# Windowed attention and an ELU layer on one core: a new start order, dummy matmuls, and scores of two groups together

## Chip, core and metric

The kernel runs on one core of a Trainium2 chip. The metric is the device time of one execution in microseconds (us). Matrix products run on TensorE (PE; PEld is its weight load), elementwise work on VectorE (DVE), ScalarE (ACT) and GpSimd (POOL); SyncE (SP), ACT and POOL also issue DMAs.

## What is computed

Attention over 8 batches, 8 heads, 576 positions and 64 values per head, in which a position sees only its neighbours at a distance of up to 32; then a layer of 512 to 2048 values with an ELU, and one back to 512, over all 4608 tokens. Inputs and output are float32.

```python
B, H, S, D = 8, 8, 576, 64
scores = q @ k.transpose(0, 1, 3, 2) / sqrt(D)
scores = where(abs(pos[:, None] - pos[None, :]) <= 32, scores, -1e9)
attn = softmax(scores)
x = (attn @ v).transpose(0, 2, 1, 3).reshape(B * S, H * D)
h = x @ w_in                                  # 4608 x 2048
g = where(h > 0, h, exp(minimum(h, 0)) - 1)
out = g @ w_out                               # 4608 x 512
```

## The kernel before

**Units, groups and tiles.** Attention is cut into units of 64 query positions, 9 per batch and 72 in all; a group `G[i]` is two neighbouring units (37 groups, since the first two batches end with a single one). A group goes through these steps. `QK` makes the scores (16 matmuls for two units, contracting over 64 partitions, even heads on partitions 0-63 and odd heads on 64-127) into the PSUM tile `psS` of two banks. `SM` takes the exponentials of the whole tile on ACT (L406). `MK` multiplies by the band masks on DVE (L419). `AV` multiplies by v, with a column of ones for the sum (`psO`, L431). `RN` divides by the sum (L445, L447), and `X` transposes the result to `xt`, through PSUM and a copy (`XT`, `X`) for the first nine groups and by a DMA transpose afterwards.

The layer takes tiles of units, `sizes = [2, 2, 2, 3, 4, 3] + [8] * 7`. `H` is the hidden product (L487) into `psH`, which has three banks; `pack` of the small tiles puts several blocks of 128 hidden values into one bank. `EX` takes the exponential on ACT (L496), `FF` forms its negative part on ACT or DVE (`fact` chooses; L506, L508), and `GG` joins both to `g_sb` on DVE (L514, L517). `Y` is the output product in four parts for each chunk of 128 tokens (L532), alternately into `psY` and `psT` from chunk 6 on; `YC` copies it on ACT and `OUT` stores it. The eight PSUM banks are: psS 2, psO 1, psT 1, psH 3, psY 1.

**Loads.** SP loads q, k and v in blocks `L(b, nm, j)` of up to 128 positions, float32, into staging tiles (`stg`, four for v; `stp`, four for pairs of k and q). Casts to bfloat16 are `CV` for v and `C`, `C2` for k and q. For batch 0 the first half of k and q is transposed on TensorE (`T`) and copied out (`TT`, by `E`). The second half of batch 0 and all of batch 1 come in another way: POOL issues casting DMAs (`LR`) which put runs of six positions on one partition, 48 partitions per half of the heads; `TR` transposes them on TensorE in pieces of 48 by 64, and `ER` copies them to their place. Batch 0 takes 4 such transfers, batch 1 takes 8. From batch 2 on, SP's DMA transposes (`XB`) do it. The weights are cast by POOL's DMAs too, in four chunks each (`WI` for w_in, `WO` for w_out). Chunk c of w_in serves hidden blocks 4c to 4c+3, chunk c of w_out part c of each output chunk.

**What sets the order.** Every step is an operation of a planner, `Plan`, with an engine, an estimated duration, a rank, dependencies, and counted resources (PSUM banks, staging tiles, a ring of SP transfers, eight POOL transfers at a time). The planner plays the program through with its estimates: whenever an engine is free it takes the ready operation of lowest rank. The order in which operations start in that play is the order in which instructions are written, and each engine and queue then runs its own in that order. Ranks follow the unit (`PER = 4` per unit); attention has `LEAD = 36` ahead of the hidden layer, 9 units. POOL's queue at the start is the list `LINE` (L636): identity, masks, a `wait` (a one-element copy that reads a loaded block, `GATE`, L643: v's block 0), then weights and `LR`. SP's first eleven loads follow `FIRST` (L634). A small memset, `GT`, holds back the loads of batch 1 until a w_out chunk is in, and those of batch 2 until a k transfer of batch 1 is in.

Of the kernel before, what the change touches and what calls it, by code (L numbers as in the profile page):

```python
# [20 lines left out]
class Plan:  # L21
# [12 lines left out]
    BEGIN = {"POOL": 1.35, "SP": 0.8}  # L34
    QLAT = {"S": 1.2, "A": 1.2, "P": 2.2}

    def __init__(self, held):
        self.ops = {}
        self.held = dict(held)
        self.acq, self.rel, self.late = {}, {}, {}  # L40

    def op(self, name, eng, dur, rank, deps, fn, dma=None, acq=None,
           rel=None, late=0.0):
        assert name not in self.ops, name
        self.late[name] = late
        self.ops[name] = (eng, dur, rank, tuple(deps), fn, dma)
        if acq:
            self.acq[name] = acq if isinstance(acq, list) else [acq]
        if rel:
            self.rel[name] = rel  # L50

    def run(self):
# [7 lines left out]
        free, ready = {}, {}  # L60
        for n, o in ops.items():
            free.setdefault(o[0], self.BEGIN.get(o[0], 0.7))
            ready.setdefault(o[0], {})
            if left[n] == 0:
                ready[o[0]][n] = 0.0
# [4 lines left out]
        import heapq  # L70

        held = dict(self.held)

        def finish(n, t):
            done[n] = t
            if n in self.rel:
                r, k = self.rel[n]
                held[r] += k
                for e in free:
                    heapq.heappush(events, (t + self.LAT, 1, e))  # L80
            for u in users.get(n, ()):
                left[u] -= 1
                if left[u] == 0:
                    ue = ops[u][0]
                    r = max(done[d] + (0.0 if ops[d][0] == ue and ops[d][5] is None
                                       else self.LAT) for d in ops[u][3])
                    ready[ue][u] = r
                    heapq.heappush(events, (max(r, t), 1, ue))

        now = 0.0  # L90
        for e in free:
            heapq.heappush(events, (free[e], 1, e))
        while len(order) < len(ops) or events or any(rings.values()):
# [4 lines left out]
            if nxt is not None and (te is None or now + nxt <= te):  # L98
                now += nxt
                for q in rings.values():  # L100
                    if q:
                        q[0][1] -= nxt / per
                        if q[0][1] <= 1e-9:
                            h = q.pop(0)
                            for a, k in self.acq.get(h[0], ()):
                                if a == "ring":
                                    held[a] += k
                                    for e in free:
                                        heapq.heappush(events, (now, 1, e))
                            heapq.heappush(events, (now + self.DLAT + self.late[h[0]],  # L110
                                                    0, h[0]))
# [7 lines left out]
            _, kind, x = heapq.heappop(events)  # L119
# [13 lines left out]
            cand = [(ops[n][2], n) for n, r in rs.items() if r <= now + 1e-9  # L133
# [3 lines left out]
            n = min(cand)[1]  # L137
# [7 lines left out]
            heapq.heappush(events, (free[e], 1, e))  # L145
            if dma is not None:
                ring, pk, ns = dma
                heapq.heappush(events, (now + self.QLAT[ring], 2, (
                    ring, [n, float(pk), ns / 1000.0])))
            else:  # L150
                lag = self.PLAT - self.LAT if e == "PE" else 0.0
                heapq.heappush(events, (now + dur + lag, 2, n))
# [3 lines left out]
        self.start, self.done, self.order = start, done, order  # L156
        for n in order:
            ops[n][4]()
# [3 lines left out]
def kernel(  # L162
# [23 lines left out]
    RUN = 6  # L186
    HT = S // (2 * RUN)
# [10 lines left out]
    NXT = 3  # L198
    NST = 4
# [52 lines left out]
    def L(b, nm, j, eng):  # L252
# [7 lines left out]
        live["L", b, nm, j] = t  # L260


    def GT(b, nm, j):
        t = room(b, nm, j)
        nc.vector.memset(t[96:97, 0:1], 0.0)
        live["G", b, nm, j] = t
# [4 lines left out]
    def WAIT(b, nm, j):  # L271
        nc.gpsimd.tensor_copy(spot[64:65], live["L", b, nm, j][64:65, 0:1])
# [70 lines left out]
    def runs(b, nm, half):  # L343
        x = "kq".index(nm) + 2 * half
        n = HP * RUN * D
        if b == 0:
            o = (4 + 2 * "kq".index(nm) + 8 * half) * GC
            t = g_sb.rearrange("p a c -> p (a c)")[:, o:o + n]
        elif x == 3:
            t = qkT[2][:, 1].rearrange("p a c -> p (a c)")[:, 0:n]  # L350
        else:
            t = vw[2].rearrange("p a h d -> p (a h d)")[:, x * n:x * n + n]
        return t.rearrange("p (a r d) -> p a r d", a=HP, r=RUN)

    def LR(b, nm, half, two):
        src = SRC[nm][b].rearrange("(a two) s d -> two a s d", two=2)[two][
            :, half * (S // 2):(half + 1) * (S // 2)]
        nc.gpsimd.dma_start(
            out=runs(b, nm, half)[64 * two:64 * two + HT].rearrange(
                "p a r d -> p a (r d)"),  # L360
            in_=src.rearrange("a (p r) d -> p a (r d)", r=RUN))

    def TR(b, nm, half, part, bank):
        pool = {"psH": psH_p, "psT": psT_p}[bank]
        pt = pool.tile([128, 2, RUN, HT], BF16, name=bank, tag=bank)
        src = runs(b, nm, half)
        for a in range(2):
            for r in range(RUN):
                for p0 in (0, 64):
                    nc.tensor.transpose(  # L370
                        pt[p0:p0 + 64, a, r, :],
                        src[p0:p0 + HT, 2 * part + a, r, :],
                        ident[p0:p0 + HT, p0:p0 + HT])
        live["TR", b, nm, half, part] = pt

    def ER(b, nm, half, part, eng):
        w = qT[b] if nm == "q" else kT[b][:, :, WIN:WIN + S]
        dst = w[:, 2 * part:2 * part + 2, half * (S // 2):(half + 1) * (S // 2)]
        copy(eng, dst.rearrange("p a (g r) -> p a g r", r=RUN),
             live.pop(("TR", b, nm, half, part)).rearrange("p a r g -> p a g r"))  # L380
# [8 lines left out]

    def QK(i):  # L390
        psS = psS_p.tile([128, 2, 2, HP, QB], FP32, name="psS", tag="psS")
        for s, u in enumerate(G[i]):
            b, qb = divmod(u, NQB)
            for h in range(H):
                hp, base = h // 2, 64 * (h % 2)
                nc.tensor.matmul(  # L396
                    psS[:, h % 2, s, hp, :],
# [3 lines left out]
        live["S", i] = psS  # L401

    def SM(i):
        pu = pup.tile([128, 2, 2, HP, QB], BF16, name="pu", tag="pu")
        n = len(G[i])
        nc.scalar.activation(pu[:, :, 0:n], live.pop(("S", i))[:, :, 0:n],  # L406
                             AX.Exp, scale=SCALE)
        live["U", i] = pu
# [12 lines left out]
    def AV(i, g):  # L421
# [3 lines left out]
        else:  # L425
            o = psO_p.tile([128, HP, VW], FP32, name="psO", tag="psO")
# [8 lines left out]
        live["O", i, g] = o  # L435

# [30 lines left out]
    def XE(i):  # L467
        dst, pt = live.pop(("XT", i))
        nc.scalar.copy(dst, pt)
# [29 lines left out]
    def fact(t, fo):  # L499
        return fo // pack(t) % 2 == 1 if t < NTA else fo % 4 != 1  # L500
# [47 lines left out]
    for t, n in enumerate(sizes):  # L548
        for u in range(p0, p0 + n):
            tof[u] = t  # L550
            if u == G[gof[u]][0]:
# [6 lines left out]
    LL, CC, XX = 36, 18, 14  # L558
    RING, XBT = 2.2, 1.3
    LATE = {("L", 0, "v", 3): 5.0, ("L", 0, "v", 4): 5.0}  # L560
# [3 lines left out]
              "sp": NSP, "cb": NCB, "swq": 8, "ring": RING})  # L564
# [18 lines left out]
    def prank(i):  # L583
        return PER * G[i][0] - LEAD

# [36 lines left out]
    for i in range(NVB):  # L622
        P.op(("zvw", i), "DVE", 1.1, -1970 + i if not i else -910 + i,
             [("TR", 1, nm, half, part) for nm in "kq" for half in range(2)
              for part in range(2)] if i == 2 else [], lambda i=i: z_vw(i))
# [3 lines left out]
    def group_of(b, nm, j):  # L629
        if nm == "q":  # L630
# [5 lines left out]
    LINE = [("id",), ("mask",), ("wait",), ("WI", 0), ("WI", 1), ("0kB",), ("0qB",),  # L636
            ("WI", 2), ("WI", 3), ("WO", 0), ("WO", 1),
            ("WO", 2), ("1kA",), ("1qA",), ("WO", 3), ("1kB",), ("1qB",)]
    CVE = {(0, 0): "DVE", (0, 1): "ACT", (1, 0): "DVE", (1, 1): "ACT",
           (1, 2): "DVE", (2, 0): "ACT", (2, 1): "ACT", (2, 2): "DVE",  # L640
           (3, 0): "DVE", (3, 1): "ACT", (3, 2): "ACT", (4, 0): "DVE",
           (4, 2): "ACT"}
    GATE = ("v", 0)  # L643
    rk = -2000.0
    for x in LINE:
        rk += 1
        if x[0] == "wait":
            P.op(x, "POOL", 0.1, rk, [("L", 0) + GATE], lambda: WAIT(0, *GATE))
# [8 lines left out]
        else:  # L657
            b, nm, half = int(x[0][0]), x[0][1], "AB".index(x[0][2])
            for two in range(2):
                P.op(("LR", b, nm, half, two), "POOL", 0.6, rk + 0.1 * two, [("wait",)],  # L660
                     lambda b=b, nm=nm, half=half, two=two: LR(b, nm, half, two),
# [232 lines left out]
```

## Time and profile before

| | |
|---|---|
| median of 3 runs | 323.94 us (323.45 to 326.56) |
| the profiled execution | 323.2 us, span of its instructions 321.4 us |
| PE busy | 298.2 us, 93% of the span, 2867 matmuls |
| DVE, ACT, POOL busy | 201.0 (63%), 215.7 (67%), 109.1 us (34%) |
| first matmul | 5.38 us |
| last matmuls | end at 317.6 us |
| chain that ended last | PE 75%, DMA 14%, DVE 4%, issue 3%, ACT 2% |
| SP's queue | 142304 packets, 35.53 MB |
| POOL's queue | 6720 packets, 5.97 MB |

The page divides the span into 40 slices of 8 us; a digit is the busy share of an engine in tenths. A busy PE may still be slow inside: its matmuls are pipelined, and at a lower clock they last longer. Some matmul records are missing in a trace, so that a group of four may show as three. POOL's casting DMAs are counted with the bytes that they write, half of what they read.

### The profile page before, as it was taken

The numbers are of one execution on the slowest core, as the hardware profiler recorded it, in microseconds if no ns is written. First come the engines' busy times: TensorE is split into PE (matmuls) and PEld (weight loads), VectorE is DVE, ScalarE is ACT, GpSimd is POOL, SyncE is SP. The second block draws the span as 40 slices with busy tenths as digits, with TensorE's granted clock in tenths as the row PEclk, the third lists the DMA queues.
The fourth block names the chain that finished last, engine by engine and source line by source line (L and its number), as shares of the span: only waits on it lengthen the run. The fifth ranks groups of instructions, "written<-read, shape, count | busy, mean of one in ns | idle before, by whom it ended". The sixth has DMA issues, their size and how long they took to land.

```text
span 321.4 us, 7525 instructions
## 1 busy us (share of the span) xinstructions
PE 298.2 (93%) x2867; PEld 166.8 (52%) x2908; DVE 201.0 (63%) x447; ACT 215.7 (67%) x357; POOL 109.1 (34%) x160
## 2 busy tenths in 40 slices
PE   1698799999999998999999999999999999999995
PEld 1486666677754454444444444444444444444442
DVE  5755768797856698566666667667666666444400
ACT  4659565577867786866677777766777766667611
POOL 3642337855445543545346434552000000000000
PEclk9999999999999999999999999999999999999999
DMA  8999999999999989989999898997111111100021
GB/s 192 184 197 206 197 207 232 216 207 186 197 235 206 271 161 192 223 181 229 173 246 213 202 216 216 219 210 168 52 50 51 49 51 51 46 35 33 34 100 65
DMA packets 154244, 51.42 MB, mean 160 GB/s; under 512 B 143200, under 2 KB 149600, under 8 KB 154208
## 3 DMA queue, kind: packets, MB, share of 16 engines
q1 hardware_dynamic: 142304, 35.53, 58.5%
q0 software_dynamic: 6720, 5.97, 11.5%
q10 hardware_dynamic: 5184, 9.44, 8.5%
q8 instruction: 23, 0.38, 0.5%
q14 instruction: 13, 0.11, 0.1%
HBM read 36.70 MB, written 9.44 MB: 144 GB/s over the span
## 4 chain that ended last, share of the span: by engine, by line
PE 75%; DMA 14%; DVE 4%; issue 3%; ACT 2%; another core or an unknown queue 1%; SPq 1%; POOL 0%; ACTq 0%; DVEq 0%; POOLq 0%
PE psH L487 32%; PE psY L532 19%; PE psT L532 14%; DMA w_out_sb<-in_moe_w_out_dram 5%; PE psO L431 5%; DMA vw<-in_k_dram 4%; DMA w_in_sb<-in_moe_w_in_dram 3%; PE psS L396 3%; DMA st<-in_v_dram 1%; PE psO L532 1%; DVE g_sb L514 1%; DVE pm L419 1%; DVE xs L447 1%; DMA xt<-xs 1%
## 5 line engine op out<-in xcount | busy, mean ns | idle before, releaser
L487 PE MATMUL psH<-xt,w_in_sb 128*128 128x512 bf16 (+3 forms) x824 | 148.6, 317 | 1.4 <-DVE qk L278 0.5
L496 ACT ACTIVATE e<-psH 128x512 f32<-128x512 f32 (+1 forms) x148 | 86.1, 585 | 72.7 <-PE psH L487 63.2
L487 PEld LDWEIGHTS <-w_in_sb 128*128 128x128 bf16 x832 | 70.6, 100 | 48.2 <-issue 1.3
L514 DVE SCALAR_TENSOR_TENSOR g_sb<-f,psH 128x512 bf16<-128x512 bf16 (+1 forms) x106 | 70.2, 665 | 24.5 <-ACT f L506 23.9
L532 PEld LDWEIGHTS <-g_sb 128*128 128x128 bf16 x576 | 53.3, 98 | 58.7
L532 PE MATMUL psY<-w_out_sb,g_sb 128*128 128x512 bf16 x299 | 78.7, 379 | 2.1 <-issue 1.3
L278 POOL CAST vw<-st 64x512 bf16<-64x512 f32 (+3 forms) x98 | 62.8, 641 | 22.1 <-DMA st<-in_v_dram 16.9
L506 ACT ACTIVATE f<-e 128x512 bf16<-128x512 f32 (+1 forms) x106 | 65.5, 618 | 2.6
L419 DVE TENSOR_TENSOR pm<-pu,masks 128x512 bf16<-128x512 bf16 x72 | 35.2, 528 | 34.7 <-ACT pu L406 34.7
L532 PE MATMUL psT<-w_out_sb,g_sb 128*128 128x512 bf16 x213 | 55.0, 379 | 1.4 <-issue 1.3
L278 POOL CAST cb<-sp 128x1024 bf16<-128x1024 f32 (+1 forms) x30 | 31.7, 1056 | 65.5 <-DMA sp<-in_q_dram 60.3
L406 ACT ACTIVATE pu<-psS 128x1024 bf16<-128x1024 f32 (+1 forms) x37 | 36.9, 996 | 3.9 <-PE psS L396 3.8
L431 PEld LDWEIGHTS <-pm 128*128 128x128 bf16 x576 | 26.9, 99 | 17.0 <-DVE pm L419 3.6
L431 PE MATMUL psO<-vw,pm 128*128 128x65 bf16 x552 | 29.9, 195 | 2.4 <-DVE pm L419 1.6
L447 DVE TENSOR_TENSOR xs<-psO,rc 128x256 bf16<-128x256 f32 (+1 forms) x71 | 30.1, 424 | 2.5
L517 DVE TENSOR_TENSOR g_sb<-psH,f 128x512 bf16<-128x512 f32 (+1 forms) x42 | 28.5, 678 | 3.2
L445 DVE RECIPROCAL rc<-psO 128x4 f32<-128x4 f32 (+1 forms) x71 | 12.9, 182 | 24.4 <-PE psO L431 24.1
L508 DVE TENSOR_SCALAR f<-e 128x512 bf16<-128x512 f32 (+1 forms) x42 | 20.4, 488 | 6.1 <-ACT e L496 6.1
L396 PEld LDWEIGHTS <-qk 64*128 64x128 bf16 x576 | 11.1, 96 | 12.9 <-issue 11.4
L396 PE MATMUL psS<-qk 64*128 64x64 bf16 x576 | 15.4, 194 | 1.2 <-DVE qk L278 0.5
L538 ACT COPY y<-psY 128x512 f32<-128x512 f32 x20 | 11.4, 572 | 5.8 <-PE psY L532 5.8
L276 ACT COPY qk<-psH 128x576 bf16<-128x576 bf16 (+2 forms) x10 | 5.8, 590 | 7.9 <-PE psH L370 3.9
(52 smaller groups left out, 84.6 us busy)
## 6 DMA issues: line engine op xcount, KB each, us to landing
out_dram<-y ACTq DMA_DIRECT2D x36, 256.0 KB, 2.6
sp<-in_k_dram SPq DMA_DIRECT2D x26, 256.0 KB, 3.9
sp<-in_q_dram SPq DMA_DIRECT2D x26, 256.0 KB, 4.0
st<-in_v_dram SPq DMA_DIRECT2D x24, 256.0 KB, 4.1
st<-in_v_dram SPq DMA_DIRECT2D x16, 192.0 KB, 3.9
w_in_sb<-in_moe_w_in_dram POOLq DMA_DIRECT2D x4, 512.0 KB, 12.0
w_out_sb<-in_moe_w_out_dram POOLq DMA_DIRECT2D x4, 512.0 KB, 16.2
sp<-in_k_dram SPq DMA_DIRECT2D x6, 128.0 KB, 3.2
```

Source lines behind the costliest of these rows:

```text
L278: eng.tensor_copy(dst, src)
L396: nc.tensor.matmul(psS[:, h % 2, s, hp, :], lhsT=kT[b % NKB][base:base + 64, hp, qb * QB:qb * QB + 128], rhs=qT[b % NKB][base:base + 64, h ...
L406: nc.scalar.activation(pu[:, :, 0:n], live.pop(("S", i))[:, :, 0:n], AX.Exp, scale=SCALE)
L419: nc.vector.tensor_mul(dst, pu[:, :, s], mb)
L431: nc.tensor.matmul(o[:, j, :], lhsT=p[:, h, s * QB:s * QB + 128], rhs=vw[b % NVB][:, qb, h, :], start=(s == 0), stop=(s == len(G[i]) - 1))
L447: nc.vector.tensor_mul(live["X", i][0:n, g * HP:(g + 1) * HP, :], o[0:n, :, 0:D], rb)
L487: nc.tensor.matmul(ps[:, f], lhsT=w_in_sb[:, do, (fo + f) * 128:(fo + f + 1) * 128], rhs=xts[t][:, do, :], start=(do == 0), stop=(do == ND ...
L496: nc.scalar.activation(e, ps, AX.Exp)
L506: nc.scalar.activation(f, e, AX.Relu, bias=1.0, scale=-1.0)
L514: nc.vector.scalar_tensor_tensor(g_sb[:, fo:fo + pack(t), gcols(t)], f, -1.0, ps, ALU.mult, ALU.max)
L517: nc.vector.tensor_tensor(g_sb[:, fo:fo + pack(t), gcols(t)], ps, f, ALU.max)
L532: nc.tensor.matmul(ps, lhsT=g_sb[:, fo, gc:gc + 128], rhs=w_out_sb[:, fo, :], start=(fo == 0), stop=(fo == NFO - 1))
```

## The change

- *Ranks.* A table `SHIFT` adds a number to the rank of some 120 operations, among them the first loads, the weights, transposes, and many hidden and output products. Ties go by the order of definition, and a dependency on TensorE counts 0.28 us in the plan where the release of a bank now counts at the end of the matmul.
- *Start.* `GATE` becomes q's block 0. In `LINE` with its shifts, the second half of q and k of batch 0 (`0k`, `0q`) comes first after the wait, then chunks of w_in and w_out in the order w_in 3, w_out 2, w_in 2, w_in 0, w_out 0, w_in 1, w_out 1, w_out 3, then batch 1. On SP the first loads sort by their new ranks (-1989 for v's block 4, -1965 for v's 1, -1959 for q's 1, -1907 for v's 2, -1899.4 for q's 0, -1899 for k's 0, v's 0 and v's 3, -1895 for k's 1, -1893, -1892).
- *Casts.* Of v of batch 0, blocks 3 and 4 and parts of 0 and 2 are cast on POOL, also q's block 2. A table `ENG` sets the engine of some copies and of some `FF`.
- *Dummies.* Where the plan has TensorE idle before 30 us, `fill` writes matmuls of the identity with itself into columns 384 to 511 of the psO bank, one for each 0.11 us.
- *Batch 1.* k and q come in one transfer each, with runs of nine positions on all 128 partitions; `TR` then has pieces of 64 by 64, 144 transposes instead of 192.
- *Twins.* From group 13 on, every second group is a twin: its scores are made directly behind those of the group before it, into psT (even heads) and one psH bank (odd heads), and its exponentials are taken in two instructions.
- *Other.* The copy `XE` of two groups goes to DVE; `GT` reads which load is first from the plan.

```diff
+    WARM = 30.0
...
-        self.ops[name] = (eng, dur, rank, tuple(deps), fn, dma)
+        self.ops[name] = (eng, dur, rank + self.shift.get(name, 0), tuple(deps),
+                          fn, dma)
...
+        pe = 2.2
         for n in order:
+            if ops[n][0] == "PE":
+                if start[n] < self.WARM:
+                    self.fill(max(0, int((start[n] - pe - 0.15) / 0.11)))
+                pe = start[n] + ops[n][1]
             ops[n][4]()
...
-    RUN = 6
-    HT = S // (2 * RUN)
+    RUNS = [(6, S // 12), (9, S // 9)]
...
+    NTW = 13
...
+    def LR(b, nm, two):
+        t, r, g = runs(b, nm)
+        src = SRC[nm][b].rearrange("(a two) (p r) d -> two p a (r d)", two=2, r=r)
+        if b:
+            src = SRC[nm][b].rearrange("(a two) s d -> a (two s d)", two=2).rearrange(
+                "a (p x) -> p a x", x=r * D)
+            t = t.rearrange("p a r d -> p a (r d)")
+        else:
+            src = src[two, g:2 * g]
+            t = t[64 * two:64 * two + g].rearrange("p a r d -> p a (r d)")
+        nc.gpsimd.dma_start(out=t, in_=src)
...
+    def twin(i):
+        return i >= NTW and (i - NTW) % 2 == 1
+
     def QK(i):
-        psS = psS_p.tile([128, 2, 2, HP, QB], FP32, name="psS", tag="psS")
+        if twin(i):
+            ps = [psT_p.tile([128, 2, HP, QB], FP32, name="psT", tag="psT"),
+                  psH_p.tile([128, 2, HP, QB], FP32, name="psH", tag="psH")]
+        else:
+            psS = psS_p.tile([128, 2, 2, HP, QB], FP32, name="psS", tag="psS")
+            ps = [psS[:, 0], psS[:, 1]]
...
+    def fill(n):
+        if "W" not in live and n:
+            live["W"] = psO_p.tile([128, 512], FP32, name="psO", tag="psO")
+        for _ in range(n):
+            nc.tensor.matmul(live["W"][:, 384:512], lhsT=ident, rhs=ident,
+                             start=True, stop=True)
...
+    SHIFT = {
+        ("zvw", 2): 926, ("WI", 0): 54, ("WI", 1): 60, ("WI", 2): 47, ("WO", 0): 49, ("WO",
+        1): 57, ("LR", 1, "k", 0): 107, ("LR", 1, "q", 0): 110, ("WO", 3): 61, ("L", 0, "k",
+        0): 100, ("L", 0, "k", 1): 103, ("L", 0, "q", 0): 97.6, ("L", 0, "v", 0): 97, ("L",
+        0, "v", 1): 30, ("L", 0, "k", 2): 100, ("L", 0, "q", 1): 35, ("L", 0, "v", 2): 85,
+        ("L", 0, "q", 2): 99, ("C", 0, "q", 2): -1931, ("L", 0, "v", 3): 91, ("L", 1, "v",
...
-    LATE = {("L", 0, "v", 3): 5.0, ("L", 0, "v", 4): 5.0}
+    LATE = {("L", 0, "v", 3): 1.0, ("L", 0, "v", 4): 1.0}
...
-    LINE = [("id",), ("mask",), ("wait",), ("WI", 0), ("WI", 1), ("0kB",), ("0qB",),
+    LINE = [("id",), ("mask",), ("wait",), ("WI", 0), ("WI", 1), ("0k",), ("0q",),
             ("WI", 2), ("WI", 3), ("WO", 0), ("WO", 1),
-            ("WO", 2), ("1kA",), ("1qA",), ("WO", 3), ("1kB",), ("1qB",)]
+            ("WO", 2), ("1k",), ("1q",), ("WO", 3)]
...
-    GATE = ("v", 0)
+    GATE = ("q", 0)
...
+        two = not twin(i) and i + 1 < NG and twin(i + 1)
+        if two:
+            for u in G[i + 1]:
+                deps += tdeps(u)
+            P.op(("QK", i), "PE", 0.66, r, deps, lambda i=i: (QK(i), QK(i + 1)),
+                 acq=[("psS", 1), ("psT", 1), ("psH", 1)])
+        elif not twin(i):
+            P.op(("QK", i), "PE", 0.43, r, deps, lambda i=i: QK(i), acq=("psS", 1))
...
+        if twin(i):
+            P.op(("SM", i, 0), "ACT", 0.55, r - PER, deps, lambda i=i: SM(i, 0),
+                 rel=("psT", 1))
+            P.op(("SM", i), "ACT", 0.55, r - PER, [("SM", i, 0)],
+                 lambda i=i: SM(i, 1), rel=("psH", 1))
```

## The prediction

> **What bounds the kernel now.** I read the page's summary of 40 slices first, then four windows of the start and the long middle (columns: stretch, length, then busy us and instructions of PE, PEld, DVE, ACT, POOL, granted clock, DMA share, GB/s):
>
> ```profile
> PE   1698799999999998999999999999999999999995
> 0.00:16.00 16.00, 6.39 (x89) 4.89 (x90) 10.35 (x34) 8.54 (x14) 8.22 (x21) 1.00 0.98 188
> 16.00:32.00 16.00, 14.01 (x280) 12.16 (x277) 8.94 (x24) 12.40 (x20) 5.08 (x8) 1.00 1.25 202
> 32.00:48.00 16.00, 13.43 (x282) 10.72 (x286) 11.35 (x26) 10.21 (x18) 5.57 (x10) 1.00 1.24 203
> 64.00:300.00 236.00, 231.27 (x1900) 120.46 (x1932) 154.54 (x330) 169.50 (x282) 77.20 (x103) 1.00 0.76 157
> ```
>
> From 64 us on TensorE is busy 98% and is the bound. Before that it is not, and the DMAs carry the start. The chain of waits in order of time (start, duration, what), and three rows of the timeline:
>
> ```profile
> 8.23 10.17 DMA w_in_sb<-in_moe_w_in_dram
> 18.69 15.06 DMA w_out_sb<-in_moe_w_out_dram
> 34.03 12.51 DMA vw<-in_k_dram
> ...
> 7.81 27.29 SPq L257 DMA_DIRECT2D st<-in_v_dram  x5
> 15.92 1.90 PE L487 MATMUL psH<-xt,w_in_sb 128*128 128x128 bf16 x16
> 24.72 0.42 DVE L278 CAST vw<-st 128x512 bf16<-128x512 f32 x1
> 25.38 1.07 PE L487 MATMUL psH<-xt,w_in_sb 128*128 128x128 bf16 x16
> ```
>
> The v blocks issued from 7.81 were overtaken by the weights: the first is cast only at 24.72. The same 16 matmuls take 1.90 us at 15.92 and 1.07 at 25.38: TensorE ran at half rate until about 20.8 (48 of them from 18.45 take 4.04 us), although the page's clock row shows full grant throughout.
>
> Busy time hides this, so I count useful work: weight loads of each line in each window, times the spacing of such a matmul in a dense stretch. Spacings: hidden layer 56 ns at 128 columns (16 in 0.90 us from 34.40 to 35.30), 82 ns at 192; output 216 (4 in 0.864); scores 27 (16 in 0.43); values 30 (8 in 0.24); batch-0/1 transposes 18 (48 in 0.87); the other transposes 40 to 56. In 0-16 that makes 3.0 us of work, in 16-32 10.7 (112 hidden, 96 transposes, 40 scores), in 32-64 27.7 (88 + 40 hidden, 44 output, 72 scores, 77 values, 192 transposes). Lost: 13.0 + 5.3 + 4.3 = 22.6 us by 64. This is what the start can give back; in the middle only the price of the work itself can fall.
>
> **What the skill says.** "TensorE: Matmul & The Clock Gate", the HAM clock gate: the array runs at 1.2 GHz until about 3.4 us of sustained activity and falls back after such a stretch of idleness; its Part 4 says that transposes do not count as activity. The 1.90 against 1.07 us agrees; the page's clock row doesn't. "TensorEngine Tiling (Array Packing)", Key Properties: "Changing tiling mode (not just tile) drains the TensorE". Scores use 64-row tiles, and the trace agrees, as priced below. "DMA: Bandwidth & Descriptors", Queues, rings and completion order: each DMA engine takes turns between queues packet by packet, so SP's small packets starve beside the weights; the v block cast at 24.72, 17 us after its issue, agrees.
>
> **The change, part by part.**
>
> *Loads and gate.* On SP the shifted ranks of batch 0 sort to v4, v1, q1, v2, q0, k0, v0, v3, k1, k2, q2 (4 `st` buffers allow it, as v4 is cast early); before it was k0, k1, q0, v0, v1 ... The weights' gate moves from v0 (fourth) to q0 (fifth). SP alone moves 266 to 271 GB/s in the 1.5 us slices of 3 to 6 us. v0 ended 0.98 MB of loads and landed at 6.66: 1.9 + 0.98/0.265 + 1.06. The same rule: q0 ends 1.25 MB, landing at 7.7; k1 ends 2.23 MB, at 11.4. All scores wait for k1 through cast, transposes and copy; before, k0 and k1 landed by 4.96 and their copies ended at 7.10, so 2.1 us later: first scores at 13.5 instead of 8.8. That loses 4.5 us more at the front. In return all of v is there by about 12 instead of 24.7 and 30.6.
>
> *POOL's queue.* Behind the gate come 4 transfers of the second half of q, k of batch 0, then w_in chunk 3, w_out 2, w_in 2, w_in 0, w_out 0, w_in 1, w_out 1, w_out 3, then k and q of batch 1. The gate is 1 us later. The half-batch transfers, landing at 20 to 22 before, land at 12 to 14. From 8.2 to 48.5 the two queues moved 13.2 MB of float32 input, 0.34 MB/us (4.19 each for w_in and w_out, 1.18 + 2.36 in half and batch transfers, the rest v). At that rate the last w_in chunk, 7.5 MB after 9.5 us, lands near 31 (27.6 before), w_out chunk 3 near 37 (27.89 + about 16 before), batch 1 near 47 as before. POOL stalled for landings from 15.17 to 37 since 8 transfers were out; now four small ones come first and free their slots early.
> Casts on POOL: v4's two and one of v2 stand ahead of the gate, 0.64 us each from the casts' row; the last may delay all weights by 0 to 0.5 us. The cast of v0's other half stands behind eight issues (4 x 0.59 + 4 x 0.75 = 5.4 us after 8.0, so 14.0); the first values need it at 13.5 + 0.65 + 1.02 + 0.76 = 15.9: hidden.
>
> *Dummies.* They fill planned TensorE gaps below 30 us at 0.11 us each, ordinary matmuls. With the clock up before the scores, 16 hidden matmuls save 1.90 - 0.90 = 1.0 and the 48 save 4.04 - 2.69 = 1.35, the attention pieces up to 3. Warm they take half of their gap, so I cost the delay of real work at 0 (0 to 0.5); their bank is psO, in columns nobody reads.
>
> *Start, summed.* Until 13.5 lost 13.5 - 0.7 of transposes = 12.8. From there to 32: 0 at best, 6.1 at the old rate (5.3/16); with full clock and all of batch 0 there by 14, but 3/4 of the hidden layer until 31, I take 3. In 32-64: old 4.3, at best 1; I take 2.3. Sum 18.1, a gain of 4.5 (from 9 to -2).
>
> *Batch 1 in 2 transfers instead of 8.* Transposes fall from 192 x 18 ns = 3.5 us to 144 x 19 = 2.7: 0.7 gained (0 to 1). The eight copies stay. POOL issues 2 instead of 8.
>
> *Two groups of scores in one go*, from group 13: 12 pairs. The rows of the middle:
>
> ```profile
> 186.55 1.03 PE L487 MATMUL psH<-xt,w_in_sb 128*128 128x512 bf16 x4
> 187.51 0.41 PE L396 MATMUL psS<-qk 64*128 64x64 bf16 x16
> 188.11 1.02 ACT L406 ACTIVATE pu<-psS 128x1024 bf16<-128x1024 f32 x1
> 188.72 1.03 PE L487 MATMUL psH<-xt,w_in_sb 128*128 128x512 bf16 x4
> 189.01 0.63 ACT L506 ACTIVATE f<-e 128x512 bf16<-128x512 f32 x1
> 190.25 0.67 DVE L514 SCALAR_TENSOR_TENSOR g_sb<-f,psH 128x512 bf16<-128x512 bf16 x1
> ```
>
> Between the two hidden starts lie 2.17 us: hidden and output 0.864 each, so scores cost 0.44. Sixteen within a block are (0.41 - 0.19)/15 apart, 0.235 in all; 0.2 is the switch. Twelve switches saved are 2.4 us. The second group sits in psT and one of three psH banks until its exponentials run, placed 4 rank units (some 4 us) after the first's. In the row above a hidden result holds its bank from 186.55 to 190.92, 4.4 us; two banks supply one per 2.2 us against a need of one per 1.96: 0.24 short each, two of them per pair, 0.5. Output matmuls need no psH bank and can step in; I let them fill most of it and charge 0.07 per pair, 0.8 in all. Net 1.6 (2.4 at best; the other end is the last rival but one). ACT adds 2 x 0.588 - 1.02 = 0.16 per pair, hidden at 67% load.
>
> *The rest* (memsets and gates of later batches moved, copies exchanged between ACT and DVE, ranks, the planner's lag): DVE 63%, ACT 67% busy, batch 2 needed first at 68.13; 0, from -1 to 1.
>
> Sum: 4.5 + 0.7 + 1.6 = 6.8 us. Against the profiled span of 321.4 that is 314.6; that execution reported 323.2, the median is 323.94: 317.1.
>
> **Rivals.** *No gain at the start*: the later k1 and the w_in chunk at 31 cost what warmth and earlier v give; queues are fixed, so one block behind its plan stalls TensorE. For it speaks the lost 4.5 at the front; against it 5.3 us of idle with operands missing in 16-32. Only scores and transposes gain: 323.9 - 2.3 = 321.6. *The dummies don't hold the clock* (issued long before the work, or idle windows follow): 2.3 of the gain go, 319.4. *Slower: the second group's psH bank.* If ACT reaches its exponentials late, each hidden result also waits behind 1.18 us more of ACT: hold 5.6, two banks supply one per 2.8, 0.84 short each. Two short per pair cost 1.7, less 0.2 saved: 1.5 x 12 = 18, less 5.2 from elsewhere: 337; at 1.0 per pair 329. It decides from (5.2 + 3.2)/12 + 0.2 = 0.9 us of TensorE idle per pair. Against it: the output matmuls, as said. *Larger gain*: start at its best, 312.
>
> **How the numbers follow.** My forecast 0.54, larger gain 0.06, no start gain 0.17, clock not held 0.12, bank stall 0.11. A measurement here can tell about 1%, 320.7 to 327.2. Faster: 0.54 + 0.06 + 0.12 less the edge = 0.71; same 0.17; slower 0.12. The range from 312 to 325 leaves out the bank stall's upper part and the best start's tail.
>
> **What would show it.** First scores near 13.5; 16 hidden matmuls in about 1.0 us from the first on; hidden work on chunk 3 first; by 64 us about 18 us lost; scores in blocks of 32 with 0.65 us between neighbours, 12 times; PE idle after 100 us not above today's 2%. Wrong if k1 lands after 16, if hidden matmuls wait on DVE in every pair, or if batch 2's scores wait for loads.

## The result, and the profile after

The changed kernel takes 319.96 us (median of 5 runs, 319.64 to 321.52) against 323.94 before: 0.9876 of the time before, 95% interval 0.983 to 0.9923. In a second set of runs, beside later experiments, it took 319.28 us, ratio 0.9841 (0.9803 to 0.9878). So 4.0 to 5.2 us are gained where 6.8 were forecast. The profiled execution, at 321.52 us, is the longest of its five, and its k block 1 came late; where a typical execution is wanted, I read the profile of the second set of runs (320.2 us, span 318.5) and call it "the repeat".

The page's rows of busy tenths and granted clock, of the changed kernel, 8 us to a slice:

```profile
PE   7499999999899999999999999999999999999995
PEclk9958999999999999999999999999999999999999
```

TensorE now looks full from 16 us on, which was the aim. But the clock row, all nines before, has a 5 and an 8 in just these slices. The windows of the changed kernel (stretch, length, then busy us and instructions of PE, PEld, DVE, ACT, POOL, granted clock, DMA share, GB/s):

```profile
0.00:16.00 16.00, 9.54 (x131) 8.70 (x131) 7.41 (x25) 4.42 (x7) 10.83 (x25) 1.00 0.97 192
16.00:32.00 16.00, 15.42 (x320) 13.61 (x320) 11.93 (x33) 9.45 (x15) 6.15 (x10) 0.68 1.24 207
32.00:48.00 16.00, 15.69 (x225) 12.37 (x224) 12.17 (x24) 11.47 (x22) 2.86 (x5) 1.00 1.07 198
64.00:300.00 236.00, 233.38 (x1950) 120.58 (x1951) 160.29 (x340) 169.89 (x290) 77.80 (x104) 1.00 0.75 157
```

From 16 to 32 us TensorE is busy 15.42 us against 14.01 before, at 0.68 of its clock: busy and slow. From 32 to 48 it gained: 15.69 against 13.43. The chain of waits of the changed kernel (start, duration, what):

```profile
7.62 6.55 DMA sp<-in_k_dram
14.19 0.44 DVE cb L297
14.67 0.40 PE psH L337 x4
...
16.18 1.40 PE psH L393 x24
17.59 0.54 PE psO L484 x4
...
20.46 0.76 DVE qk L297
21.22 1.26 DVE pm L459 x2
22.61 0.44 DVE xs L497
23.09 0.81 PE psO L484 x6
...
26.84 0.89 PE psH L537 x16
```

The weights, w_in and w_out, which carried the chain of before from 8 to 34 us, are gone from it. In their place stand k's block 1 until 14.19, and then TensorE itself, with dummies (L484) among its links, broken from 20.46 to 23.05 by VectorE: a copy of transposed q and k, two masked exponentials and a division. In the repeat the chain waits for k's block 2 instead, the load behind block 1: 6.38 us from 8.51, cast at 14.92.

Now the same count of useful work as in the prediction (weight loads of each line in a window times the dense spacing), made again in finer windows and in the same way for each kernel. Lost us, cumulated (time gone by less useful work done):

| up to | before | after | repeat | without dummies |
|---|---|---|---|---|
| 16 us | 12.8 | 14.6 | 14.3 | 13.9 |
| 32 us | 18.5 | 20.7 | 19.9 | 19.5 |
| 64 us | 23.7 | 22.6 | 21.8 | 22.3 |
| 100 us | 23.9 | 23.9 | 23.2 | 22.6 |
| 300 us | 26.0 | 24.3 | 23.7 | 24.1 |

The prediction's 22.6 for before by 64 us is 23.7 in this count. Most of the difference lies in its 32 to 64 us: the pieces that it lists there make 25.4 us at its own spacings, some 26.4 with the 20 transposes of x that the list leaves out, and not 27.7. In the repeat the start brings 23.7 - 21.8 = 1.9 us by 64; from 64 to 100 it loses 1.3 where before lost 0.2, so 1.1 goes back; from 100 to 300 it loses 0.5 where before lost 2.1, a gain of 1.6; and 0.7 us of transposes are not there any more. Sum 3.1, against 321.4 - 318.5 = 2.9 between the two spans. The medians differ by more than these two executions do; from run to run, the spans of both kernels scatter by 2 to 3.5 us. The counts are estimates, good to about half a microsecond, since the widths of the hidden products are mixed.

Where the start's time went is seen in the repeat's timeline of TensorE from its first scores to its first hidden product (start, us, engine, line, operation, out<-in, count; in brackets the idle before and its releaser):

```profile
13.59 0.60 PE L431 MATMUL psS<-qk 64*128 64x64 bf16 x16
15.39 0.28 PE L337 MATMUL psH<-ident,cb 32*128 32x32 bf16 x4 [1.21 <-DVE cb L297]
15.60 1.48 PE L393 MATMUL psH<-ident,g_sb 48*64 48x48 bf16 x48
17.01 0.61 PE L484 MATMUL psO<-ident 128*128 128x128 bf16 x4
...
18.54 0.61 PE L431 MATMUL psS<-qk 64*128 64x64 bf16 x16
19.08 0.84 PE L393 MATMUL psH<-ident,g_sb 48*64 48x48 bf16 x24
19.85 0.71 PE L484 MATMUL psO<-ident 128*128 128x128 bf16 x5
20.62 0.60 PE L472 MATMUL psO<-vw,pm 128*128 128x65 bf16 x8
...
22.55 0.80 PE L484 MATMUL psO<-ident 128*128 128x128 bf16 x6 [0.35 <-DVE xs L497]
...
24.85 0.41 PE L431 MATMUL psS<-qk 64*128 64x64 bf16 x16
...
25.77 1.06 PE L537 MATMUL psH<-xt,w_in_sb 128*128 128x128 bf16 x16
```

Sixteen scores take 0.61 us at 18.54 and 0.41 at 24.85; 48 transposes take 1.48 us where the dense price is 0.87. These 12.18 us hold, at full-rate prices, 64 scores (1.73), 40 values (1.20), 96 transposes of 48 rows (1.73), 8 small ones (0.40) and 4 of x (0.22): 5.28 us. The dummies, each group from its start to the start of what follows, take 0.54 + 0.77 + 0.85 + 0.09 + 0.34 = 2.59. Idle time is 1.21 + 0.35 = 1.56; the 1.21 are the wait for the cast of k's block 2. The rest, 2.75, is put down to the lower clock; it is what is left over, not a measurement of its own. The granted clock of the repeat in these windows (stretch, length, PE busy and instructions, clock, DMA share, GB/s):

```profile
12.00:14.00 2.00, 1.00 (x25) 1.00 1.17 181
14.00:16.00 2.00, 0.79 (x27) 0.62 1.17 169
16.00:18.00 2.00, 2.00 (x58) 0.50 1.25 196
...
22.00:24.00 2.00, 1.60 (x25) 0.50 1.22 201
24.00:26.00 2.00, 1.94 (x44) 0.82 1.24 206
```

The array runs at half rate from about 14.5 to 24.7 us (worked out from the shares in the windows), in spite of the dummies, and in a stretch where the chain of waits runs for the most part through TensorE.

The pairs look as priced. TensorE of the changed kernel around one of them:

```profile
181.41 1.03 PE L584 MATMUL psY<-w_out_sb,g_sb 128*128 128x512 bf16 x4
182.37 0.41 PE L431 MATMUL psS<-qk 64*128 64x64 bf16 x16
182.61 0.19 PE L431 MATMUL psT<-qk 64*128 64x64 bf16 x1
...
182.94 2.76 PE L584 MATMUL psY<-w_out_sb,g_sb 128*128 128x512 bf16 x12
```

The four output products end at 181.41 + 0.864 = 182.27, the next ones begin at 182.94: 32 scores in 0.67 us, where two groups took 2 x 0.44 before. Behind them stand twelve output products that need no psH bank, as the prediction supposed.

### The profile page after: what moved, and what is told of

Same layout as the page of the kernel before. It is cut to its first block, busy times and chain, and to the rows that moved or that the text cites. A ratio compares the mean times of both kernels' runs of the same rounds, so it can differ in the third digit from the quotient of the medians.

```text
span 319.8 us, 7692 instructions
## 1 busy us (share of the span) xinstructions
PE 305.9 (96%) x2974; PEld 172.3 (54%) x2974; DVE 206.4 (65%) x451; ACT 210.1 (66%) x357; POOL 111.6 (35%) x162
## 4 chain that ended last, share of the span: by engine, by line
PE 79%; DVE 8%; ACT 6%; DMA 2%; SPq 2%; issue 2%; ACTq 0%; DVEq 0%
PE psH L537 32%; PE psY L584 19%; PE psT L584 15%; PE psO L472 5%; ACT e L546 3%; DMA sp<-in_k_dram 2%; SPq L271 2%; DVE pm L459 2%; ACT f L558 2%; DVE g_sb L566 2%; PE psS L431 2%; PE psH L393 2%; DVE f L560 1%; PE psS L584 1%; PE psO L584 1%
## 5 line engine op out<-in xcount | busy, mean ns | idle before, releaser
L537 PEld LDWEIGHTS <-w_in_sb 128*128 128x128 bf16 x832 | 68.8, 98 | 51.7 <-issue 3.0
L297 POOL CAST vw<-st 64x512 bf16<-64x512 f32 (+2 forms) x105 | 68.0, 649 | 45.9 <-DMA st<-in_v_dram 40.1
L584 PE MATMUL psY<-w_out_sb,g_sb 128*128 128x512 bf16 x320 | 80.8, 379 | 0.0
L584 PE MATMUL psT<-w_out_sb,g_sb 128*128 128x512 bf16 x224 | 56.8, 379 | 0.0
L297 POOL CAST cb<-sp 128x1024 bf16<-128x1024 f32 (+2 forms) x31 | 32.2, 1039 | 64.1 <-DMA sp<-in_q_dram 60.7
L459 DVE TENSOR_TENSOR pm<-pu,masks 128x512 bf16<-128x512 bf16 x72 | 37.9, 568 | 5.9 <-ACT pu L444 4.3
L472 PEld LDWEIGHTS <-pm 128*128 128x128 bf16 x576 | 26.9, 100 | 16.0 <-DVE xs L497 2.9
L444 ACT ACTIVATE pu<-psS 128x1024 bf16<-128x1024 f32 (+1 forms) x25 | 24.6, 984 | 12.9 <-PE psS L431 12.5
L484 PE MATMUL psO<-ident 128*128 128x128 bf16 x114 | 11.2, 266 | 1.8 <-POOL ident masks.py:199 1.4
L431 PE MATMUL psS<-qk 64*128 64x64 bf16 x384 | 10.7, 197 | 0.0
## 6 DMA issues: line engine op xcount, KB each, us to landing
w_in_sb<-in_moe_w_in_dram POOLq DMA_DIRECT2D x4, 512.0 KB, 12.9
```

Source lines behind the costliest of these rows:

```text
L297: eng.tensor_copy(dst, src)
L431: nc.tensor.matmul(ps[h % 2][:, s, hp, :], lhsT=kT[b % NKB][base:base + 64, hp, qb * QB:qb * QB + 128], rhs=qT[b % NKB][base:base + 64, hp ...
L459: nc.vector.tensor_mul(dst, pu[:, :, s], mb)
L472: nc.tensor.matmul(o[:, j, :], lhsT=p[:, h, s * QB:s * QB + 128], rhs=vw[b % NVB][:, qb, h, :], start=(s == 0), stop=(s == len(G[i]) - 1))
L537: nc.tensor.matmul(ps[:, f], lhsT=w_in_sb[:, do, (fo + f) * 128:(fo + f + 1) * 128], rhs=xts[t][:, do, :], start=(do == 0), stop=(do == ND ...
L584: nc.tensor.matmul(ps, lhsT=g_sb[:, fo, gc:gc + 128], rhs=w_out_sb[:, fo, :], start=(fo == 0), stop=(fo == NFO - 1))
```

## The experiments

After the trace three explanations stood for the smaller gain: the late k block 1 holds the scores, and all behind them; the dummies cost time of their own, or fail to hold the clock; or the order of TensorE's queue sets the first hidden product, whatever comes earlier. The pairs, the other large term, had to be priced alone, and so had the transfers of batch 1. Ratios below are to the kernel before on the same chip, whose median was 324.3 to 324.7 us.

**Without the pairs.**

```diff
-    NTW = 13
+    NTW = 99
```

> The changed kernel with every group's scores made alone again (twins start at group 99, so there are none); all else stays. Theory A, the pairs are worth their switches and cost no bank stalls: the middle's period for two groups was 15.67 us before and is 15.37 with pairs, so 12 x 0.2 to 0.3 come back, 2.4 to 3.6: 322.4 to 323.6 us. Rival B, the second group's banks give the saving back: 319.5 to 320.5, as with pairs.

Measured 321.6 us, ratio 0.9915 (0.9888 to 0.9942). The changed kernel's ratios, 0.9876 and 0.9841, are lower by 0.0039 and 0.0074 of 324 us: the pairs are worth 1.3 to 2.4 us there, where 1.6 was forecast. The first set's interval overlaps with this one, the second set's does not. The time lies between the two that were expected.

**Without the dummies.**

```diff
-    WARM = 30.0
+    WARM = 0.0
```

> The changed kernel without the dummy matmuls; the order of everything else is the same. Theory A, the clock that the dummies raise is lost again before the scores (TensorE stood idle from 12.0 to 14.7 us, and scores at 15.3 to 25.4 run 0.61 us a block as on a slow clock): the dummies are worth 0 to 0.7, 320.0 to 320.7 us, and the hidden layer starts slow or not much later. Rival B, they do hold the clock for the hidden layer: without them the first 64 hidden matmuls cost 2.3 more, 322 us.

Measured 318.92 us, ratio 0.9833 (0.9802 to 0.9864): not slower than with them, and below both times that were expected. The interval overlaps with those of the changed kernel, so that a gain isn't settled either. Its timeline of TensorE:

```profile
13.96 0.40 PE L431 MATMUL psS<-qk 64*128 64x64 bf16 x8
...
15.11 1.48 PE L393 MATMUL psH<-ident,g_sb 48*64 48x48 bf16 x48
...
19.07 0.62 PE L472 MATMUL psO<-vw,pm 128*128 128x65 bf16 x8
...
23.71 1.90 PE L537 MATMUL psH<-xt,w_in_sb 128*128 128x128 bf16 x16
25.54 0.40 PE L431 MATMUL psS<-qk 64*128 64x64 bf16 x8
```

From first scores to first hidden product 9.75 us instead of 12.18: the same 5.28 of work, no dummies, 0.92 idle, 3.55 from the low clock. The hidden products come 2.1 us earlier, but the first sixteen take 1.90 instead of 1.06. The same transposes take 1.48 and 0.84 us with and without dummies, so at this place the dummies warm nothing. The clock row of this execution is full throughout, as it was before; that it is in fact at half rate until about 26.9 (eight values take 0.62 us at 25.87, where they take 0.40 at the full clock) is seen in the durations alone.

**Dummies packed densely.** Behind 6 us of the plan one dummy for each 0.056 us of gap instead of 0.11.

```diff
-                    self.fill(max(0, int((start[n] - pe - 0.15) / 0.11)))
+                    self.fill(max(0, int((start[n] - pe - 0.15) / (0.11 if start[n] < 6 else 0.056))))
```

> The changed kernel with twice as many dummy matmuls in gaps that the plan places after 6 us (one per 0.056 us, which is what a warm one takes). Theory A, the clock fell because the dummies, run at the full clock, filled only half of each gap: now the clock stays up from about 6 us, scores take 0.41 a block instead of 0.61, values likewise, and 1.0 to 2 us are gained: 318 to 319 us. Rival B, the clock does not matter at that place, since the pieces wait for copies anyway, or the dummies stand in front of real work: 319.7 to 321.

Measured 322.09 us, ratio 0.9922 (0.9896 to 0.9948): 2.1 us above the changed kernel's first set, whose interval overlaps, and 2.8 above the repeat, whose interval doesn't. Neither theory expected so much. Its timeline of TensorE:

```profile
15.35 0.41 PE L431 MATMUL psS<-qk 64*128 64x64 bf16 x16
...
16.05 0.94 PE L393 MATMUL psH<-ident,g_sb 48*64 48x48 bf16 x48
16.92 0.62 PE L484 MATMUL psO<-ident 128*128 128x128 bf16 x8
...
21.07 1.01 PE L484 MATMUL psO<-ident 128*128 128x128 bf16 x8 [1.80 <-issue]
22.14 0.60 PE L472 MATMUL psO<-vw,pm 128*128 128x65 bf16 x8
...
23.65 1.46 PE L484 MATMUL psO<-ident 128*128 128x128 bf16 x12
```

With gaps filled, the clock holds: scores in 0.41, 48 transposes in 0.94. In an idle stretch of 1.80 us, for which the profile names no releaser, it falls: 0.53 of full in 20 to 22 us, so from about 20.1, and it stays at 0.50 until about 26.9. From first scores to first hidden product 12.51 us: 5.28 work, 4.08 dummies, 1.80 idle, 1.35 low clock. So the dummies can hold the clock, and what they save in it (2.75 - 1.35 = 1.4 us) they cost again (4.08 - 2.59 = 1.5). They also cost before this stretch: k's block 1 was cast by 13.53, but its transposes stood behind 48 dummies (11.74 to 14.42) and began at 14.42, where the repeat's began 0.06 us after the cast. That is some 0.8 us of the first scores' delay.

**k's block 1 ahead in the ranks.** It changes places with v's block 4.

```diff
-        0): 100, ("L", 0, "k", 1): 103, ("L", 0, "q", 0): 97.6, ("L", 0, "v", 0): 97, ("L",
+        0): 100, ("L", 0, "k", 1): 9, ("L", 0, "v", 4): 94, ("L", 0, "q", 0): 97.6, ("L", 0, "v", 0): 97, ("L",
```

> The changed kernel with two of SP's first loads exchanged: k's block 1 takes the first place and v's block 4 the ninth. Theory A, the late k block is what ate the gain at the start (it landed near 14.1 us where 11.4 was reckoned): scores start at 10 to 11.5, 4 us earlier, and 2 to 4 us of it reach the end: 316 to 318 us. Rival B, the start is bound by the weights' landing, or by v4 which is now late: 319.5 to 321.

Measured 327.6 us, ratio 1.0087 (1.0055 to 1.0119). The first scores do come 2.6 us earlier than in the repeat, at 10.97, but the first values at 19.59 and the first hidden product at 25.85, 1.0 before and 0.1 behind the repeat's; by 64 us 26.8 are lost. Both theories missed. The planner writes every queue anew for the new ranks, so this run doesn't price k1 alone; a load moved by rank isn't a single edit in this kernel. It does show that early scores alone don't bring the hidden layer forward.

**The changed kernel again**, on the chip of the next three.

> The changed kernel as it is, beside the next three on the same chip, and for a second profile of it. Both theories: 319.5 to 320.5 us; k1's cast at 13 to 14.2 us, as in the other runs with this order of loads.

Measured 319.28 us, ratio 0.9841 (0.9803 to 0.9878): the repeat.

**k's block 1 ahead of v's block 0, in SP's order alone.** The move is made after the plan, so every other queue keeps its order.

```diff
         pe = 2.2
+        order.remove(("L", 0, "k", 1))
+        order.insert(order.index(("L", 0, "v", 0)), ("L", 0, "k", 1))
         for n in order:
```

> The changed kernel with one edit after the plan: k's block 1 is issued just ahead of v's blocks 0 and 3, seventh on SP instead of ninth; every other queue keeps its order exactly. Theory A, scores wait for k1 alone, and they are on the path: k1 lands 1.5 to 2 us sooner, first scores near 12.5, and 1 to 2 us reach the end: 318 to 319 us. Rival B, behind the scores the values wait anyway (for v0's cast on POOL, which stands behind POOL's transfers, and for the dummies): 319.7 to 320.5.

Measured 319.72 us, ratio 0.9865 (0.9823 to 0.9908): no gain over the repeat, as rival B had it, but its trace shows another wait than the one it named. In its profiled execution, at 322.98 us the longest of the six, the scores begin at 12.85, and then TensorE waits 2.65 us, until 16.09, for the cast of k's block 2, which had stayed where it was:

```profile
16.09 0.29 PE L339 MATMUL psH<-ident,cb 32*128 32x32 bf16 x4 [2.65 <-DVE cb L299]
```

Block 1 isn't the last load that is needed there.

**No dummies behind the first values.** `fill` returns once the first values are written, which drops some ten of them.

```diff
     def fill(n):
+        if "av" in live:
+            return
```

> The changed kernel with no dummies from the first values on; those before stay. Theory A, what makes the dummies cost 1 us is that those between the values wait until DVE has read the bank that they write to (0.6 us a time, and all TensorE work queued behind them): the hidden layer starts as early as without dummies, near 24 us, and the time is that without dummies or 0.5 better: 318.4 to 319.2. Rival B, the early ones cost it, by standing in front of the transposes and scores: 319.7 to 320.5.

Measured 319.91 us, ratio 0.9865 (0.9824 to 0.9905): no difference, as rival B had it. Yet in the profiled execution (319.46 us, span 317.8) the first hidden products begin at 23.65, near the 24 of theory A, and take 1.05 us for sixteen. That is 2.1 us ahead of the repeat's, 0.9 of it from earlier scores (12.68), but the span is only 0.7 shorter. So the earlier start of the hidden layer reached the end only in part.

**k's block 1 moved, and no dummies** (the edits of two runs together).

> Both: k's block 1 seventh on SP, and no dummies. Theory A, both lie on the way to the first hidden products and add up: 316.8 to 318 us. Rival B, one hides the other: 318.5 to 319.2, as without dummies alone.

Measured 318.59 us, ratio 0.9807 (0.977 to 0.9845): within rival B. First scores at 13.13, first hidden product at 22.88, 2.9 us ahead of the repeat's; by 32 us 18.5 are lost, by 64 us 20.2 and by 300 us 22.3, the least of the kernels counted. In time it is 0.7 us below the repeat (1.1 between the means, with intervals that overlap).

**v's block 0 cast on ACT.** Its second half, which POOL casts, goes to ACT ahead of the first exponentials; nothing else moves.

```diff
+        order.remove(("CV", 0, 0, 1))
+        order.insert(order.index(("SM", 0)), ("CV", 0, 0, 1))
...
-                         lambda b=b, j=j, part=part, eng=eng: CV(b, j, part, engs[eng]),
+                         lambda b=b, j=j, part=part, eng="ACT" if (b, j, part) == (0, 0, 1) else eng:
+                         CV(b, j, part, engs[eng]),
```

The reason for this run is POOL's timeline in the repeat:

```profile
14.11 0.79 POOL L660 DMA_DIRECT2D w_out_sb<-in_moe_w_out_dram  x1
15.01 0.74 POOL L655 DMA_DIRECT2D w_in_sb<-in_moe_w_in_dram  x1
15.79 0.60 POOL L297 CAST cb<-sp 32x512 bf16<-32x512 f32 x1
16.35 1.48 POOL L660 DMA_DIRECT2D w_out_sb<-in_moe_w_out_dram  x2
17.87 1.28 POOL L297 CAST vw<-st 64x512 bf16<-64x512 f32 x2
```

The cast that was forecast for 14.0 begins at 17.87, behind q's block 2 and two issues more.

> The changed kernel with one cast moved, all other orders kept: the second half of v's block 0 goes from POOL, where it ended at 18.5 to 19.5 us behind the transfers, to ACT ahead of the first exponentials. Theory A, the first values wait for that cast: they start 1 to 1.5 us earlier, at 19 to 19.5 with the dummies, and about 1 us reaches the end: 318 to 319. Rival B, at that time TensorE is taken up by transposes and dummies in its own order anyway: first values and time as in the changed kernel, 319.3 to 320.3.

Measured 319.08 us, ratio 0.982 (0.9791 to 0.9849), between the two times expected, and in its timeline of TensorE:

```profile
18.86 0.84 PE L395 MATMUL psH<-ident,g_sb 48*64 48x48 bf16 x24
19.63 0.72 PE L486 MATMUL psO<-ident 128*128 128x128 bf16 x5
20.40 0.60 PE L474 MATMUL psO<-vw,pm 128*128 128x65 bf16 x8
```

The values begin at 20.40, not earlier than the repeat's by more than its earlier scores explain (12.95 against 13.59). They wait for no operand: transposes and dummies stand ahead of them in TensorE's queue. The late cast wasn't what held them, and no gain from moving it is seen.

**All three together**: no dummies, k1 moved, the cast on ACT.

> No dummies, k's block 1 seventh on SP, and v0's half cast on ACT. Theory A, each takes one wait from the way to the first hidden product: values near 17.3, first hidden product near 21.5, 0.5 to 1.2 us better than the first two alone (0.981 of the time before): 317 to 318. Rival B, the cast is hidden by the transposes ahead of it: 318.2 to 318.9, as the first two alone.

Measured 318.57 us, ratio 0.9806 (0.978 to 0.9833): below the kernel before by 6 us. Its interval lies below that of the changed kernel's first set only at its edge (0.983) and overlaps with the second's (0.9803 to 0.9878); a gain of about 1 us over the changed kernel is likely and not settled. It adds nothing to the run with two of the three, as rival B had it.

**The kernel before with the pairs alone.** The edits to the scores, the exponentials and their planned operations as in the change, ranks and loads as before.

```diff
+    NTW = 13
...
+        if twin(i):
+            ps = [psT_p.tile([128, 2, HP, QB], FP32, name="psT", tag="psT"),
+                  psH_p.tile([128, 2, HP, QB], FP32, name="psH", tag="psH")]
```

> The kernel before with the pairs of scores alone, from group 13 on. Theory A, a pair saves one switch of the array, 0.2 us, 12 times, and its banks cost little: 2.0 to 2.8 us less than before, ratio 0.9915 to 0.994. Rival B, without the order that goes with it the held psH bank stalls the hidden products: ratio 0.997 to 1.005.

Measured 324.87 us, ratio 0.9997 (0.9977 to 1.0018): no gain. What is worth about 2 us in the changed kernel is worth nothing here, to within 0.7 us. In its trace, from 64 to 300 us, TensorE waits 2.6 us in all for VectorE and ScalarE, against 1.2 before; most of it is for masked exponentials (1.4 us), the rest for a read of the psO bank (0.6), for psH banks (0.4) and for exponentials (0.2). The 2.6 us of "issue" that the profile lists before stand at groups of four that show as three, so they are missing records and not waits. Longer waits fit an order which isn't made for the pairs; that they are the whole of it isn't shown.

**The kernel before with batch 1 in two transfers**, 144 transposes instead of 192. What hangs on these transfers moves with them: batch 2's loads now wait for q's.

```diff
-            ("WO", 2), ("1kA",), ("1qA",), ("WO", 3), ("1kB",), ("1qB",)]
+            ("WO", 2), ("1k",), ("WO", 3), ("1q",)]
```

> The kernel before with batch 1's k and q in one transfer each, 144 transposes instead of 192, at the same places of POOL's queue. Theory A, worth the 48 transposes, 0.7 us (0 to 1): ratio 0.997 to 1.000. Rival B, the DMAs are the bound there and 1024 descriptors instead of 1536 bring batch 1 in earlier: 1.5 us or more, ratio under 0.9955.

Measured 324.31 us, ratio 0.9986 (0.9961 to 1.001), a gain of 0.5 us with 0 and the forecast 0.7 both inside.

## Why the prediction was right in direction and too large

**The first scores at 13.5.** Right in a typical execution: 13.59 in the repeat, with 12.9 lost until then, against 12.8. In the profiled one k's block 1, issued at 7.62, was cast at 14.19, and the scores came at 15.28. The landing, put at 11.4, was 12.2 and 14.2. "DMA: Bandwidth & Descriptors", Queues, rings and completion order, in the Trainium skill has a possible reason: the engines take turns between queues, and from 8.65 us POOL's transfers stand beside it. The sum of bytes had left this out; no run takes it apart. It had also left out k's block 2, for which TensorE waits next (1.21 us in the repeat).

**The step that failed is the next one: "From there to 32 ... I take 3".** It supposed the full clock from the first scores on. The repeat loses 7.0 us there (19.9 - 12.9): 1.56 idle, 2.75 from the low clock, 2.59 in dummies, 0.1 behind the first hidden product. Two assumptions of the sum fell together. "With the clock up before the scores" held until about 14.5 us and no longer. And "I cost the delay of real work at 0 (0 to 0.5)" was an amount for dummies in idle time; but from 15 us on TensorE had transposes, scores and values queued behind them, and its plan's gaps were no gaps on the chip. The runs show both sides: without dummies the same stretch is 2.4 us shorter, and its like transposes are as slow; with dense ones the clock holds until 20.1 instead of 14.5 and the stretch is no shorter (12.51 us).

The rival "the dummies don't hold the clock", at 319.4, is what happened, in its mechanism (idle windows follow them) and nearly in its time. I had given it 0.12. Its remark that 2.3 us of the gain would go is close to the 2.75 counted; the dummies' own 2.59 were in no case. That its time fits as well is in part luck: it had neither these nor the 1.1 us below, and it took what the kernel before loses as 1.1 us smaller than the later count.

**The half cast of v's block 0, "hidden".** It was to be ready at 14.0; it began at 17.87 or, if it is the second of the two casts in that row, at 18.5. (The eight issues alone end at 8.0 + 5.4 = 13.4; the 14.0 includes the cast.) "Hidden" came true for another reason: the values were themselves 4.7 us later than the forecast 15.9. POOL's queue had to be counted with q's block 2 and two more issues.

**32 to 64 us.** 2.3 was put as lost, 1.9 was, in both profiles. Here the start does pay: before lost 5.2 in the same stretch, when it waited for weights and v.

**"The rest", 0 from -1 to 1.** It cost 1.1 us from 64 to 100 us in the repeat. TensorE's waits there, in the same timeline as above:

```profile
73.28 1.03 PE L537 MATMUL psH<-xt,w_in_sb 128*128 128x256 bf16 x8 [0.46 <-DVE g_sb L569]
82.48 0.82 PE L537 MATMUL psH<-xt,w_in_sb 128*128 128x192 bf16 x8 [1.02 <-DVE g_sb L569]
```

Hidden products wait for a psH bank that VectorE has not read yet; before, TensorE's only idle stretch there was 0.16 us. VectorE has 67 operations and 29.09 us in this stretch against 59 and 27.20, but the copies moved to it aren't enough as a cause: without dummies it has the same 67 (28.34 us), and TensorE waits for it 0.18 us only and loses 0.3 there instead of 1.3. Why the repeat waits longer stays open.

**The pairs.** Net 1.6 was forecast, from 12 switches saved less 0.8 for short banks. There are 12 pairs, 0.67 us each (0.65 forecast); the count gives 1.6 in 100 to 300 us, the run without them 1.3 to 2.4. The bank stall, the slower rival, did not come: TensorE is busy 196.90 of 200 us there in the repeat, against 195.80 before in a trace with as many records. What the price missed is that it belongs to an order, not to the pair: on the kernel before it is 0, to within 0.7 us.

**The transposes of batch 1.** 0.7 forecast, 0.5 (-0.3 to 1.3) measured alone.

Term by term for the repeat: start 4.5 forecast and 1.9 found, transposes 0.7 and 0.7 (counted at the forecast price), pairs 1.6 and 1.6, the rest 0 and -1.1. The time lies within the range because that reached to the rivals. Of what was to be shown, the first sixteen hidden products in about 1.0 us (1.06) and an idle TensorE behind 100 us no longer than before came true; "by 64 about 18 us lost" did not.

What stays open: why the pairs give nothing on the kernel before; what TensorE waits for from 64 to 100 us with the dummies and not without; what the 1.80 us of the dense dummies wait for (they end 0.14 us after VectorE's masked exponentials, which the values behind these dummies read, but the profile doesn't tie the two); and whether the last microsecond between the changed kernel and the one with three edits is real.

## What to carry to other kernels

Price dummy matmuls as work: where real instructions queue behind them they delay these, and half-filled gaps did not keep the clock. Before costing a stretch at full rate, ask in which part of it TensorE will be busy without a break, and read the rate from the durations of like instructions rather than from a clock row. An operand that comes earlier gains only if no other operand is as late (k's block 2 behind block 1) and if the engine's own queue lets it; where orders are fixed ahead, look first at what stands in front of the waiting instruction.

## What the runs showed of the hardware

The clock fell sooner than I had thought from the skill. "TensorE: Matmul & The Clock Gate", The HAM clock gate, names an idle window of about 3.4 us; in the repeat TensorE was idle for 1.62 us until 12.98 and again from 14.2, and the rate halved at 14.5; in the changed kernel's first profile it was idle for 2.68 us until 14.67, and the rate halved at 16.0; with dense dummies it halved at 20.1, within an idle stretch that began at 19.3. So no unbroken idle time of 3.4 us was needed. What exactly is counted the runs don't show: in the 3.4 us before these three falls, dummies and scores filled 1.2, 1.0 and 1.3 us, and idle time and transposes the rest. In the dense run transposes took more of it (1.3 us) than idle time (0.8), so its fall can't be put down to the idle stretch alone. That page's word that transposes don't count as activity agrees with the run without dummies, where TensorE worked almost without a break from 15.11 to 20.1 us, mostly on transposes, and stayed at half rate until about 26.9, 3.2 us into its hidden products.

A granted clock below 1 goes with longer runs. The 23 runs of the changed kernel, its repeat, the one with k1 moved and the one with fewer dummies list mean clocks over the whole run:

| mean clock | runs | median us |
|---|---|---|
| 1.0 | 2 | 318.3 |
| 0.988 to 0.989 | 8 | 319.4 |
| 0.982 to 0.984 | 10 | 320.4 |
| 0.977 to 0.979 | 3 | 321.9 |

From 1.0 to 0.978 it is 0.022 x 318 / 0.5 = 14 us at half rate, and the runs are 3.6 us longer. The 23 runs are of three slightly different kernels, so this is a relation and not a price. The changed kernel without dummies, in its three forms, lists 0.998 to 1.0, though its matmuls are slow at the start: in these profiles the row shows a fall only after the array has once been fast.
